# A diffusion ResBlock on one core: outer rows added by accumulating transfers in three more chunks, a wider weight nest, another order in the last unit

## The chip, the cores and the metric

The kernel runs on one core of one Trainium2 chip. The metric is the device time of one execution in microseconds, the median of several runs. A program's instructions go to TensorE (PE in the profile, its weight loads PEld), VectorE (DVE), ScalarE (ACT), GpSimd (POOL) and SyncE (SP). Each engine works through its own instructions in the order in which they stand in the program, and waits at an instruction whose inputs another engine has not finished. SP and POOL also issue transfers by the DMA engines; a transfer that adds to what lies at its destination is issued by POOL here.

## The reference

```python
# B, C, H, W = 2, 512, 64, 64; E = 1152; all inputs bfloat16
def gn(z, gamma, beta):                 # 4 groups of 128 channels, eps 1e-5
    zr = z.reshape(B, G, (C // G) * H * W)
    mu = zr.mean(-1).reshape(B, G, 1)
    var = ((zr - mu) ** 2).mean(-1).reshape(B, G, 1)
    zn = ((zr - mu) / jnp.sqrt(var + eps)).reshape(B, C, H, W)
    return zn * gamma.reshape(1, C, 1, 1) + beta.reshape(1, C, 1, 1)
def conv3(z, w):                        # 3x3, padding 1, the sum of nine taps
    zp = jnp.pad(z, ((0, 0), (0, 0), (1, 1), (1, 1)))
    taps = [jnp.einsum("bchw,oc->bohw", zp[:, :, i:i+H, j:j+W], w[:, :, i, j])
            for i in range(3) for j in range(3)]
    return sum(taps)
h = conv3(silu(gn(x, g1, be1)), w1)
h = h + (silu(t_emb) @ w_emb).reshape(B, C, 1, 1)
h = conv3(silu(gn(h, g2, be2)), w2)
return x + h
```

Two group norms, two 3x3 convolutions of 512 channels to 512 channels on two images of 64 x 64, an embedding and a residual.

## The kernel before

**The convolution.** It isn't computed tap by tap. Along the rows of the image it goes by a fast scheme: an output tile of four rows (at four interleaved positions) is made from six transformed planes of the input and six transformed weights. Planes 0 to 3 are the "middle points" and planes 4 and 5 the "outer points": plane 4 and plane 5 each give a part that belongs to only one of the four outputs (8 rows of the 32 that a chunk has, rows 24 to 31 and rows 0 to 7 of the tile as it is laid out). Along the columns a second, two-point nest saves a third of the matmuls of the middle points. VectorE makes the planes ("rows_a", "rows_b") from the activated input, and from the raw weights it makes the transformed ones.

**Chunks and units.** A chunk is one layer, one image and one half of the image's rows: eight chunks, 0 to 3 for the first convolution and 4 to 7 for the second. A unit is one chunk and one of four blocks of 128 output channels: 32 units, and their matmuls follow each other on TensorE in a fixed chain (`chain=True` in `mm`). A unit of chunks 4 to 6 has 88 matmuls: twelve of 512 columns for plane 4, 16 of 256 (B, points 0 and 2), twelve for plane 5, 16 (B, points 1 and 3), 16 (A, 0 and 2), 16 (A, 1 and 3). Chunk 7 nests the outer points too (Bo and Ao), so that all its 96 matmuls have 256 columns.

**After the matmuls.** ScalarE evacuates PSUM into float16 tiles: `evac_o` takes an outer point from bank 6 or 7 into the buffer OO, `evac_b` and `evac_pair` take two banks of the middle points (M, BT). PSUM has eight banks: 6 and 7 for the outer points, three pairs in turn for the middle ones. VectorE adds the B part (S, A in the names), takes sums and differences (s, d), ScalarE or VectorE scales (8, 2, 4), VectorE writes the 32 rows of the result to a buffer YS (y), and then the outer points are added to its rows 0 to 7 and 24 to 31 (O). There are two YS, used in turn, and in chunks 4 to 6 two OO, also in turn, at an offset in the weight regions (L970).

**How the outer points are added.** `CFG['oacc']` (L298) says it by chunk. Where it is 1 (chunks 0 to 2), one accumulating transfer on POOL's queue adds OO into YS; where it is 0, VectorE does it, in chunks 4 to 6 in two additions of 520 elements per partition (8 rows of 65):

```python
if CFG["oacc"][c] and not last:
    dma(yo.ap, oo.ap, [oo, yo], [yo], P * 4 * PL, nm + "oa", sw=True, acc=True)
elif md == "1":
    for i, r0 in ((1, 0), (0, 24)):
        r = A(ys + r0 * RW, [[1, PL]])
        tt(r, r, A(OO[i], [[1, PL]]), AD, nm + "O")
```

A unit of the second layer then stores YS to the output by another accumulating transfer on POOL's queue; the residual has been copied there before.

**The last chunk.** Before each unit of chunk 7, `nest_st` (L882) makes the nested weights of the outer points from the raw ones in six VectorE additions of 512 elements; the last of each half overwrites part of the raw weights. `unit7` (L890) runs B 0,2; B 1,3; the sums S of both; A 0,2; A 1,3; Bo; Ao. For the very last unit `last_y` (L1110) takes the place of the ending: it adds the residual x on VectorE, adds plane 5 straight from PSUM (L1142) and stores in three pieces on SP's queue.

**The order.** The whole program is recorded as a list of operations with planned durations, on five resources (PE, DVE, ACT, POOL, DMA). A list scheduler (`Plan._run`) then takes, at each step, the ready operation with the best priority, which fixes the order of every engine; `emit` writes the instructions in the order of planned start. The priorities come from a backward pass, corrected by a table of names (NUDGE) and by thirty seeded random moves (ORDER). POOL's transfers share a planned DMA resource with SP's, but on the chip they stand in POOL's own order, between its memsets.

Of the kernel before, what the change touches and what calls it, by code (L numbers as in the profile page):

```python
# [10 lines left out]
ACT = mybir.ActivationFunctionType  # L11
ALU = mybir.AluOpType
AX = mybir.AxisListType
F32 = mybir.dt.float32
BF16 = mybir.dt.bfloat16
# [6 lines left out]
class Op:  # L22
    __slots__ = ("i", "eng", "cost", "lat", "fn", "preds", "succs", "name", "start", "slack", "sw", "boost")


NUDGE = {
    ('a10', 'DMA'): -6.1,
    ('emb', 'DMA'): -4.9,
    ('k01', 'DVE'): 3.6,
    ('k10', 'DVE'): -17.9,  # L30
    ('ld_ur02', 'DMA'): -31,
    ('ld_ur11', 'DMA'): -12.6,
    ('ld_ur12', 'DMA'): 4.6,
    ('ld_ur13', 'DMA'): -26.7,
    ('ld_ur21', 'DMA'): -3.1,
    ('ld_ur23', 'DMA'): -69.1,
    ('ld_ur3', 'DMA'): -62.2,
    ('rob10', 'DVE'): -6,
    ('row11', 'DVE'): 19.2,
    ('silu00', 'ACT'): -8.7,  # L40
    ('silu11', 'ACT'): -0.4,
    ('st01', 'DVE'): 24.1,
    ('st02', 'ACT'): 36.2,
    ('st02', 'PE'): 26.8,
    ('st03', 'ACT'): 61.3,
    ('st10', 'ACT'): -3.4,
    ('st11', 'ACT'): -24.7,
    ('u004', 'DVE'): 81.3,
    ('u00d', 'DVE'): -4.5,
    ('u00y', 'DVE'): -1.5,  # L50
    ('u01m1', 'ACT'): -14.6,
    ('w1_00', 'DMA'): 12.8,
    ('w1_01', 'DMA'): -14.6,
    ('w1_03', 'ACT'): 45.4,
    ('w1_13', 'DVE'): 35.8,
    ('w1_20', 'DVE'): 27.3,
    ('w1_22', 'ACT'): 48.7,
    ('w1_22', 'DVE'): 67.4,
    ('w1_23', 'DVE'): 187.4,
    ('w1_31', 'ACT'): 16.7,  # L60
    ('w1_33', 'ACT'): 79.1,
}


ORDER = (2, (
    (204379228, 255, 30, 1),
    (234843898, 319, 120, 1),
    (211139775, 268, 30, 3),
    (669684967, 433, 15, 3),
    (1006773657, 341, 15, 3),  # L70
    (788794351, 91, 15, 3),
    (40166790, 349, 60, 1),
    (920935792, 232, 15, 1),
    (410399867, 107, 60, 0.3),
    (420875362, 192, 15, 1),
    (385567171, 251, 30, 3),
    (279912161, 95, 30, 0.3),
    (315890846, 329, 120, 1),
    (696499368, 218, 60, 1),
    (272137600, 194, 15, 0.3),  # L80
    (605732795, 129, 30, 1),
    (29479506, 139, 15, 1),
    (973994246, 204, 15, 1),
    (488781037, 250, 30, 1),
    (34394231, 99, 30, 0.3),
    (655024064, 49, 30, 0.3),
    (144588941, 58, 60, 0.3),
    (252865214, 352, 15, 1),
    (1046031975, 342, 30, 1),
    (242005847, 138, 15, 1),  # L90
    (974414065, 143, 15, 1),
    (73604465, 212, 30, 3),
    (659385421, 129, 15, 1),
    (738286652, 264, 120, 3),
    (573361134, 368, 15, 1),
))


class Plan:
# [118 lines left out]
    def solve(self, rounds=3):  # L218
        ops = self.ops
        n = len(ops)  # L220
        tail = [0.0] * n
        for o in reversed(ops):
            tail[o.i] = o.cost + max((tail[s] + self.edge_lat(o, ops[s]) for s in o.succs), default=0.0)
        pri = [-t for t in tail]
        pris, best = [], None
        for k in range(rounds):
            pris.append(pri)
            st, span = self._run(pri, False)
            if k + 1 == rounds:
                break  # L230
            bt, bspan = self._run([-(s + o.cost) for s, o in zip(st, ops)], True)
            pri = [-(b + o.cost) for b, o in zip(bt, ops)]
        k, moves = ORDER
        pri = np.array(pris[k]) - np.array([NUDGE.get((o.name, o.eng), 0.0) for o in ops])
        st = np.array(self._run(pri.tolist(), False)[0])
        for seed, t0, w, sg in moves:
            pri = pri + np.where((st >= t0) & (st < t0 + w), np.random.default_rng(seed).normal(size=n) * sg, 0.0)
        best = self._run(pri.tolist(), False)
        self.span = best[1]
        for o, s in zip(ops, best[0]):  # L240
            o.start = s
        return best
# [26 lines left out]
def _idx(off, dims):  # L269
# [8 lines left out]
PL = 8 * RW  # L278
# [6 lines left out]
BB, CT, P, NCH, ET = 2, 4, 128, 2, 9  # L285
# [6 lines left out]
CFG = {  # L292
    'k0': (D_, D_, D_, D_),
    't0': D_,
    'k': (D_, D_, A_, D_, A_, A_, A_, A_),
    't': (D_, D_, A_, D_, A_, A_, A_, A_),
    's': ((D_, D_, D_), (D_, D_, D_), (D_, A_, A_), (D_, D_, D_), (A_, A_, A_), (A_, A_, A_), (A_, A_, A_), (D_, A_, D_)),
    'oacc': (1, 1, 1, 0, 0, 0, 0, 0),  # L298
    'np': 1,
    'st0': ('DA', 'DA', 'DP', 'PP'),  # L300
    'warm': 9,
    'bact': 1,
    'push': (40.0, 0.0, 0.0, 0.0),
    'vacc': (0, 1, 1, 1, 1, 1, 1, 0),
# [4 lines left out]
def kernel(  # L309
# [14 lines left out]
    o = 0  # L324
    UREG, UM = [], 10304
# [57 lines left out]
    def A(off, dims, dt=None):  # L383
        b = ar[:] if dt is None else ar[:].bitcast(dt)
        n = 1
        for d in dims:
            n *= d[1]
        return R(bass.AP(b.tensor, b.offset + off, [list(b.ap[0])] + [list(d) for d in dims]),
                 ("A", _idx(off, dims)), n)
# [32 lines left out]
    def tt(out, a, b, op, name=""):  # L422
        return pl.op("DVE", 0.075 + 0.000521 * out.n, lambda: nc.vector.tensor_tensor(out=out.ap, in0=a.ap, in1=b.ap, op=op),  # L423
              regs(a, b), regs(out), name)
# [40 lines left out]
    def mm(lst, name="", chain=True, slack=2.5, boost=0.0, warm=1.0):  # L465
        rr, ww, cost = [], [], 0.0
        for out, lhsT, rhs, st, sp in lst:
            rr += [lhsT, rhs]
            ww.append(out)
            cost += {512: 0.2195, 256: 0.109, 384: 0.166}.get(rhs.n, max(0.0715, rhs.n / 2330.0)) * warm  # L470

        def fn():
            for out, lhsT, rhs, st, sp in lst:
                ins = nc.tensor.matmul(out.ap, lhsT=lhsT.ap, rhs=rhs.ap, start=st, stop=sp, skip_group_check=True)  # L474
            return ins
        pl.op("PE", cost, fn, regs(*rr), regs(*ww), name, chain=chain, slack=0.0 if chain else slack, boost=boost)
# [113 lines left out]
    def st_off(s, ct):  # L590
        return UREG[2 * s + ct // 2] + 8192 + (ct % 2) * 768
# [107 lines left out]
    LV = VB[0]  # L699
# [38 lines left out]
    SB_, AD = ALU.subtract, ALU.add  # L738
# [79 lines left out]
    ucnt = [0]  # L818
# [46 lines left out]
    def Bo_mms(bank, c, k, ct, s):  # L865
        lst = []
        for q in range(2):
            w = (A(LV + 4160 + ucnt[0] % 2 * 1024 + ct * 256 + (s - 4) * 128, [[1, 128]]) if q == 0 else
                 A(st_off(ucnt[0] % 2, ct) + (s - 4) * 384 + 128, [[1, 128]]))
            lst.append((Ps(bank, q * 256, [[1, 256]]), w, A(onest(ct, 3 - q, s), [[1, 256]]),  # L870
                        ct == 0 and q == 0, ct == CT - 1 and q == 1))
        return lst
# [7 lines left out]
        return lst  # L880

    def nest_st(s, nm):  # L882
        for h in range(2):
            g = lambda kx, dt=BF16: A(st_off(s, 2 * h) + kx * 128, [[384, 4], [1, 128]], dt)
            t = A(LV + 3136 + h * 512, [[128, 4], [1, 128]])
            tt(t, g(0), g(2), ALU.add, nm)
            tt(A(LV + 4160 + s * 1024 + h * 512, [[128, 4], [1, 128]]), t, g(1), ALU.add, nm)
            tt(g(1, None), t, g(1), ALU.subtract, nm)

    def unit7(c, k):  # L890
        nm = f"u{c}{k}"
# [3 lines left out]
        last = u == 31  # L895
        BT, SD = BT1, SD1
# [5 lines left out]
        def run(steps):  # L902
            for (bank, s, fn) in steps:
                for ct in range(CT):
                    mm(fn(bank, c, k, ct, s), nm + f"{fn.__name__[0]}{s}")

        def evac_b(s, bank):
            act(A(BT + s * 512, [[1024, 2], [1, 512]]), Ps(bank, 0, [[512, 2], [1, 512]]), ACT.Copy, scale=0.5 * KAP[s], name=nm + "b")

        def evac_pair(s, bank):  # L910
            act(M(s, 2, 1024), Ps(bank, 0, [[512, 2], [1, 512]]), ACT.Copy, scale=KAP[s], name=nm + f"m{s}")

        row = lambda base, r0, dt=None: A(base + r0 * RW, [[RW, 8], [33, 2], [1, 32]], dt)
        nest_st(u % 2, nm + "n")
        run([(p1, 0, B_mms), (p1 + 1, 2, B_mms)])
        evac_b(0, p1)
        run([(p2, 1, B_mms), (p2 + 1, 3, B_mms)])
        evac_b(1, p2)
        g = lambda q: A(BT + q * 256, [[512, 4], [32, 8], [1, 32]])
        for o, op in ((0, AD), (32, SB_)):  # L920
            tt(A(SD + o, [[512, 4], [64, 8], [1, 32]]), g(0), g(1), op, nm + "S")
        run([(p3, 0, A_mms), (p3 + 1, 2, A_mms)])
        evac_pair(0, p3)
        run([(p4, 1, A_mms), (p4 + 1, 3, A_mms)])
        evac_pair(1, p4)
        run([(p5, 4, Bo_mms), (p5 + 1, 5, Bo_mms)])
        for i, sc in enumerate((0.5, 0.125)):
            act(A(BO + i * 512, [[1, 512]]), Ps(p5 + 1 - i, 0, [[1, 512]]), ACT.Copy, scale=sc, name=nm + "b")
# [17 lines left out]
        tt(A(ys, [[RW, 32], [33, 2], [1, 32]]), A(MB, [[SD - MB, 2], [0, 2], [1, 512]]),  # L946
           A(MB + 1536, [[SD - MB - 512, 2], [-512, 2], [1, 512]]), AD, nm + "y")
        yo = A(ys, [[24 * RW, 2], [1, PL]])
        tt(yo, yo, A(OS, [[PL, 2], [1, PL]]), AD, nm + "O")
        tt(yo, yo, A(OA, [[PL, 2], [1, PL]]), AD, nm + "O")  # L950
        yv = A(ys, [[1, YF]])
        b, ch = chunks[c][1:]
        dma(out[b, k, ch], yv.ap, [yv], [K("o", b, k, ch, i) for i in range(2)], P * YF * 2, nm + "out", sw=True, acc=True)
# [493 lines left out]
```

## Time and profile before

| | us |
|---|---|
| median of 5 runs | 457.53 |
| lowest and highest of them | 456.85 and 462.34 |
| the profiled execution | 456.85 |
| its span, first to last instruction | 454.8 |
| TensorE busy | 441.3 |
| VectorE busy | 432.4 |
| ScalarE busy | 391.7 |
| POOL busy | 63.4 |

The mean granted clock of TensorE is 0.992. The six transfer groups of the profile that matter here: outer rows and plane sums added in SBUF by POOL's queue, 30 transfers of 260 KB; results added to the output, 15 of 520 KB; the residual copied to the output, 30 of 260 KB; raw weights of the second layer, 28 of 192 KB; the stored activations read back, 16 of 520 KB; the last stores, one of 260 and two of 130 KB.

In the profile's rows, L423 is the line of `tt`, so all two-input VectorE operations carry it; L427 is `ts`, L446 `act`, L459 `dma`, L463 `memz`, L474 the matmuls. So one goes by shapes: 128x520 on VectorE is an outer addition of chunks 4 to 6, 128x512 from bf16 is the weight nest, 128x2048 the y rows. The columns of a group are: line, engine, operation, tiles, shapes, count | busy us, mean ns of one | idle us of the engine just before them and what ended it. Successive VectorE instructions overlap a little, so a group's busy time is less than the count times the mean.

### The profile page before, as it was taken

How to read it: one execution, taken by the hardware profiler on the slowest of the kernel's cores; microseconds unless marked ns; L12 is line 12 of the kernel's file. 1: busy time of each engine (PE TensorE's matmuls, PEld its weight loads, DVE VectorE, ACT ScalarE, POOL GpSimd, SP SyncE). 2: the span in 40 equal slices, each digit the busy share in tenths (PEclk: the TensorE clock that was granted, in tenths of full speed). 3: DMA queues.
4: the chain of work that ended last, by engine and by line, in shares of the span. 5: the costliest groups of instructions: out<-in, count | busy, mean ns of one | idle time of the engine just before them, and what ended most of it. 6: DMA issues, size and time to landing. Idle time of an engine off the chain costs nothing. (4 is left out here: it accounts for less than half of the span.)

```text
span 454.8 us, 8314 instructions
## 1 busy us (share of the span) xinstructions
PE 441.3 (97%) x2866; PEld 277.7 (61%) x2866; DVE 432.4 (95%) x865; ACT 391.7 (86%) x620; POOL 63.4 (14%) x94
## 2 busy tenths in 40 slices
PE   6899999999999999999999999999999999999993
PEld 4654444456555555555555566777666667788883
DVE  4899999999999999979999999998999999999997
ACT  5989999999999997799995899859997999567663
POOL 2110020112110221112110001121121111011211
PEclk9899999999999999999999999999999999999998
DMA  8974479979887788987996757858884864363844
GB/s 323 397 242 119 137 199 269 257 189 281 277 205 224 220 208 241 257 263 251 268 363 225 247 193 207 212 144 179 200 206 93 199 194 101 100 165 49 194 86 94
DMA packets 45977, 94.10 MB, mean 207 GB/s; under 512 B 7024, under 2 KB 18160, under 8 KB 45936
## 3 DMA queue, kind: packets, MB, share of 16 engines
q1 hardware_dynamic: 35712, 77.60, 50.9%
q0 software_dynamic: 9936, 15.98, 22.6%
q8 instruction: 22, 0.36, 0.3%
q14 instruction: 19, 0.16, 0.1%
q10 hardware_dynamic: 288, 0.01, 0.0%
HBM read 62.25 MB, written 31.32 MB: 206 GB/s over the span
## 5 line engine op out<-in xcount | busy, mean ns | idle before, releaser
L474 PE MATMUL psum<-ar 128*128 128x256 f16 (+2 forms) x2739 | 427.6, 319 | 1.5 <-DVE ar L423 1.0
L423 DVE TENSOR_TENSOR ar<-ar 128x1024 f16<-128x1024 f16 (+6 forms) x692 | 403.2, 650 | 10.3 <-ACT ar L446 6.8
L474 PEld LDWEIGHTS <-ar 128*128 128x128 f16 (+1 forms) x2775 | 267.7, 98 | 160.2 <-issue 2.5
L446 ACT ACTIVATE ar<-ar 128x512 f16<-128x512 f16 (+6 forms) x204 | 181.6, 926 | 19.2 <-DVE ar L423 15.3
L446 ACT ACTIVATE ar<-psum 128x512 f16<-128x512 f32 (+3 forms) x227 | 157.6, 726 | 31.2 <-PE psum L474 16.8
L446 ACT ACTIVATE ar<-ar,fs 128x2112 f16<-128x2112 f16 (+3 forms) x36 | 70.8, 1973 | 0.7 <-DMA ar<-in_x_dram 0.6
L459 POOL DMA_DIRECT2D ar<-ar x30 | 30.5, 1040 | 161.9 <-DVE ar L423 71.7
L459 POOL DMA_DIRECT2D out_dram<-ar x15 | 18.2, 1210 | 94.5 <-DVE ar L423 94.5
L427 DVE TENSOR_SCALAR ar<-ar 128x512 f16<-128x512 f16 (+4 forms) x74 | 24.9, 350 | 0.0
L446 ACT ACTIVATION_READ_ACCUMULATOR ar<-psum 128x1 f32 x96 | 22.0, 229 | 0.0
L463 POOL MEMSET ar<- 128x65 f16 (+6 forms) x30 | 5.9, 240 | 80.7 <-DVE ar L423 35.3
L446 ACT ACTIVATION_READ_ACCUMULATOR ar<-ar 128x1 f32 x50 | 10.5, 211 | 0.0
L474 PE MATMUL psum<-ar,ones_bf 128*128 128x260 bf16 x40 | 6.1, 303 | 2.7 <-DMA ar<-in_x_dram 2.1
L1188 DVE BATCH_NORM_STATS2 fs<-ar 128x6 f32<-128x416 bf16 x15 | 8.0, 581 | 0.0
L567 POOL TENSOR_TENSOR fs<-fs 128x4 f32<-128x4 f32 x3 | 4.0, 1347 | 21.5 <-DVE fs L555 21.5
L474 PEld LDWEIGHTS psum<-fs,ones_neg 128*128 128x128 f32 x42 | 5.7, 191 | 2.1 <-DVE fs L1192 0.7
L474 PEld LDWEIGHTS <-ones_bf 128*128 128x128 bf16 x40 | 4.1, 107 | 4.2 <-issue 2.7
L474 PE MATMUL psum<-fs,ones_neg 128*128 128x1 f32 (+3 forms) x42 | 5.4, 242 | 0.9 <-DVE fs L1192 0.6
L559 POOL TENSOR_TENSOR fs<-fs 128x1 f32<-128x1 f32 x4 | 3.0, 744 | 21.2 <-DVE fs L555 21.2
L489 PE MATMUL psum<-ones_bf 128*128 128x512 bf16 x9 | 3.6, 582 | 1.1 <-DVE ones_bf L480 1.1
L545 DVE TENSOR_SCALAR fs<-psum 128x2 f32<-128x2 f32 x4 | 0.6, 159 | 3.9 <-PE psum L474 3.4
L446 ACT ACTIVATE fs<-fs 128x1 f32<-128x1 f32 x4 | 1.5, 384 | 1.9 <-POOL fs L560 1.9
(46 smaller groups left out, 19.9 us busy)
## 6 DMA issues: line engine op xcount, KB each, us to landing
ar<-in_w_dram SPq DMA_DIRECT2D x32, 384.0 KB, 4.6
ar<-in_x_dram SPq DMA_DIRECT2D x16, 552.5 KB, 5.0
h_scr<-ar SPq DMA_DIRECT2D x16, 520.0 KB, 3.3
ar<-h_scr SPq DMA_DIRECT2D x16, 520.0 KB, 3.7
out_dram<-in_x_dram SPq DMA_DIRECT2D x30, 260.0 KB, 3.9
ar<-ar POOLq DMA_DIRECT2D x30, 260.0 KB, 4.9
out_dram<-ar POOLq DMA_DIRECT2D x15, 520.0 KB, 6.1
u_scr<-ar SPq DMA_DIRECT2D x16, 384.0 KB, 3.6
```

What stands on the lines that cost most here:

```text
L423: return pl.op("DVE", 0.075 + 0.000521 * out.n, lambda: nc.vector.tensor_tensor(out=out.ap, in0=a.ap, in1=b.ap, op=op), regs(a, b), regs(o ...
L427: pl.op("DVE", cost or 0.075 + 0.00026 * out.n, lambda: nc.vector.tensor_scalar(out=out.ap, in0=a.ap, scalar1=s, scalar2=None, op0=ALU.mul ...
L446: lambda: nc.scalar.activation(out=out.ap, in_=a.ap, func=func, scale=sc, **kw), regs(*rr), regs(*ww), name)
L459: lambda: eng.dma_start(out=out, in_=in_, **kw), regs(*r), regs(*w), name, lat=lat or (3.2 if sw else None), after=after, sw=sw)
L463: pl.op("POOL" if eng == "gpsimd" else "DVE", 0.08 + 0.0005 * out.n, lambda: e.memset(out.ap, v), (), regs(out), name)
L474: ins = nc.tensor.matmul(out.ap, lhsT=lhsT.ap, rhs=rhs.ap, start=st, stop=sp, skip_group_check=True)
L489: nc.tensor.matmul(psum[:, 0:512], lhsT=ones_bf[:], rhs=wr, start=True, stop=True, skip_group_check=True)
L545: pl.op("DVE", 0.16, lambda: V.tensor_scalar(out=F(tot, 2 * n).ap, in0=ps.ap, scalar1=YF / HW, scalar2=None, op0=ALU.mult), regs(ps), regs ...
L559: nc.gpsimd.tensor_tensor(out=N.ap, in0=N.ap, in1=F(NEGH, n).ap, op=ALU.pow)
L567: pl.op("POOL", 0.85 if n == 1 else 1.9, lambda: nc.gpsimd.tensor_tensor(out=F(rs, n).ap, in0=N.ap, in1=F(NEGH, n).ap, op=ALU.pow), regs(N ...
L1188: pl.op("DVE", 0.07 + 0.00104 * d.n, lambda d=d, i=i: V.bn_stats(out=F(BNS + 6 * i, 6).ap, in_=d.ap), regs(d), regs(F(BNS + 6 * i, 6)), name)
```

## The change

Five edits:

1. `oacc` becomes 1 for chunks 4, 5 and 6: the two additions of 520 in each of their twelve units become one accumulating transfer of 128 x 2 x 520 elements on POOL's queue.
2. `nest_st` works on all four input blocks at once: three additions of 1024 elements in place of six of 512. The third result goes to a place of its own (offset 10496), and `Bo_mms` reads it there; the raw weights are no longer overwritten.
3. In the last unit the middle points go in pairs: B 0,2; its sums; A 0,2; then B 1,3; its sums; A 1,3; Bo and Ao follow as before. The sums S are four operations of 512 elements there, in place of two of 1024.
4. The planner's priorities: the backward pass, NUDGE and ORDER go, and one number for each recorded operation stands in a table PRI. The planned duration of a 512-column matmul goes from 0.2195 to 0.2202.
5. A switch `o7` is added that could add the outer points of chunk 7 by transfer; it is (0, 0), so nothing of it is used.

```diff
-NUDGE = {
...
-ORDER = (2, (
...
+PRI = (
+    3890, 4301, 4467, 4151, 4299, 4149, 4525, 4510, 4474, 4467, 4462, 4457, 4453, 4446, 4443, 4461, 4465, 4447, 4440, 4436, 4433, 4426, 4420, 4409,
...
+)
@@ Plan.solve
-        pris, best = [], None
-        for k in range(rounds):
...
-        best = self._run(pri.tolist(), False)
+        assert len(PRI) == n
+        best = self._run([-p / 10.0 for p in PRI], False)
@@ CFG
-    'oacc': (1, 1, 1, 0, 0, 0, 0, 0),
+    'oacc': (1, 1, 1, 0, 1, 1, 1, 0),
...
+    'o7': (0, 0),
@@ mm
-            cost += {512: 0.2195, 256: 0.109, 384: 0.166}.get(rhs.n, max(0.0715, rhs.n / 2330.0)) * warm
+            cost += {512: 0.2202, 256: 0.109, 384: 0.166}.get(rhs.n, max(0.0715, rhs.n / 2330.0)) * warm
@@ Bo_mms
-            w = (A(LV + 4160 + ucnt[0] % 2 * 1024 + ct * 256 + (s - 4) * 128, [[1, 128]]) if q == 0 else
-                 A(st_off(ucnt[0] % 2, ct) + (s - 4) * 384 + 128, [[1, 128]]))
+            w = A(LV + (10496 if q else 4160) + ucnt[0] % 2 * 1024 + ct * 256 + (s - 4) * 128, [[1, 128]])
@@ nest_st
-        for h in range(2):
-            g = lambda kx, dt=BF16: A(st_off(s, 2 * h) + kx * 128, [[384, 4], [1, 128]], dt)
-            t = A(LV + 3136 + h * 512, [[128, 4], [1, 128]])
-            tt(t, g(0), g(2), ALU.add, nm)
-            tt(A(LV + 4160 + s * 1024 + h * 512, [[128, 4], [1, 128]]), t, g(1), ALU.add, nm)
-            tt(g(1, None), t, g(1), ALU.subtract, nm)
+        g = lambda kx: A(st_off(s, 0) + kx * 128, [[UM, 2], [384, 4], [1, 128]], BF16)
+        n = lambda o: A(LV + o, [[512, 2], [128, 4], [1, 128]])
+        tt(n(3136), g(0), g(2), ALU.add, nm)
+        tt(n(4160 + s * 1024), n(3136), g(1), ALU.add, nm)
+        tt(n(10496 + s * 1024), n(3136), g(1), ALU.subtract, nm)
@@ unit7
+        def s_ops(i, st, n):
+            for o, op in ((0, AD), (32, SB_)):
+                g = lambda q: A(BT + i * 512 + q * 256, [[st, n], [32, 8], [1, 32]])
+                tt(A(SD + i * 512 + o, [[st, n], [64, 8], [1, 32]]), g(0), g(1), op, nm + "S")
+
+        if last:
+            for i, b_, a_ in ((0, p1, p2), (1, p3, p4)):
+                run([(b_, i, B_mms), (b_ + 1, i + 2, B_mms)])
+                evac_b(i, b_)
+                s_ops(i, 1024, 2)
+                run([(a_, i, A_mms), (a_ + 1, i + 2, A_mms)])
+                evac_pair(i, a_)
+        else:
...
+            s_ops(0, 512, 4)
...
```

In the built program VectorE has 34 operations fewer (24 additions, 12 of the nest, and two sums more), POOL has twelve transfers more, each standing ahead of its unit's store, and TensorE has the same matmuls, in another order within the last unit. The order of the other operations differs from before in few places in the first chunks and in more of them from chunk 4 on.

## The prediction

> **What bounds the kernel now.** I read the busy shares first, then the idle time of TensorE, then of VectorE, then the end of the trace.
>
> The head of the page:
>
> ```profile
> span 454.8 us, 8314 instructions
> PE 441.3 (97%) x2866; PEld 277.7 (61%) x2866; DVE 432.4 (95%) x865; ACT 391.7 (86%) x620; POOL 63.4 (14%) x94
> ```
>
> Two engines are nearly full, so one must see where each is the limit. The timeline of TensorE alone, its last two rows (start, length, what, idle before), and its waits from 36 us on:
>
> ```profile
> 295.43 35.66 PE L474 MATMUL psum<-ar 128*128 128x512 f16 x258
> 331.56 115.96 PE L474 MATMUL psum<-ar 128*128 128x512 f16 x912 [0.47 <-ACT ar L446]
> ...
> PE psum L474 <- ACT ar L446: 0.5, 1, 0.5
> ```
>
> From 36 us to its last matmul at 447.5 us TensorE idles visibly once, 0.47 us. No matmul is added or removed. So only three places can give time: the first 36 us, that stall (with 0.08 us more between 406 and 447 us in the table by stretches), and the 7.3 us from 447.5 to 454.8.
>
> VectorE's waits, first for 323 to 452 us, then for 256 to 323 us:
>
> ```profile
> DVE ar L423 <- issue: 0.6, 1, 0.6
> ...
> DVE ar L423 <- ACT ar L446: 2.8, 4, 1.4
> ```
>
> VectorE is full through chunks 5 to 7, but it is TensorE that is never late for long: VectorE's queue is long, not limiting. That changes at the end. The timelines there, ScalarE, then VectorE, then the output transfers:
>
> ```profile
> 444.06 1.51 ACT L446 ACTIVATE ar<-psum 128x1024 f16<-128x1024 f32 x2 [0.72 <-PE psum L474]
> 445.81 0.60 ACT L446 ACTIVATE ar<-psum 128x512 f16<-128x512 f32 x1 [0.23 <-PE psum L474]
> 446.69 0.60 ACT L446 ACTIVATE ar<-psum 128x512 f16<-128x512 f32 x1 [0.28 <-PE psum L474]
> 447.32 1.92 ACT L446 ACTIVATE ar<-ar 128x512 f16<-128x512 f16 x3
> ...
> 442.69 8.43 DVE L423 TENSOR_TENSOR ar<-ar 128x1024 f16<-128x1024 f16 x18
> 451.04 0.68 DVE L1142 TENSOR_TENSOR ar<-ar,psum 128x512 bf16<-128x512 f16 x1
> ...
> 449.32 2.76 SPq L459 DMA_DIRECT2D out_dram<-ar  x3
> ```
>
> VectorE ends at 451.72, 4.2 us after TensorE, and the last store and the program's end take 3.1 us more.
>
> **The change, part by part.** Durations come from one execution of 456.85 us (span 454.8 and 2.05 around it); the median of five is 457.53, 0.68 more.
>
> *Outer rows by transfer.* In each of the 12 units of chunks 4 to 6, two VectorE additions go and one accumulating transfer on POOL's queue comes. The groups:
>
> ```profile
> L423 DVE TENSOR_TENSOR ar<-ar 128x520 f16<-128x520 f16 x60 | 24.4, 423 | 0.1
> L459 POOL DMA_DIRECT2D ar<-ar x30 | 30.5, 1040 | 161.9 <-DVE ar L423 71.7 <-issue 20.9 <-PE psum L474 20.9
> ar<-ar POOLq DMA_DIRECT2D x30, 260.0 KB, 4.9
> ```
>
> VectorE's instructions overlap: 692 of 0.650 us are 449.8 us, but L423 is busy 403.2 us, so each costs 0.067 less than its length, 0.36 us for this form. 24 x 0.36 = 8.6 us leave VectorE. Nearly all of it lies beside TensorE and is worth nothing there by itself. What it can do is remove the stall. At 331.56 TensorE waited for ScalarE, and ScalarE waits for VectorE 22.1 us in 21 places between 256 and 447 us, against 12.9 us for TensorE. With VectorE earlier by 0.7 us per unit I count both stalls as gone: **-0.55 us** (bounds 0 and -0.55).
>
> The price is a new wait. The buffer of the outer rows (OO, two sets) is written again two units later by the opening evacuation (o4) on ScalarE. Before, it was free when VectorE had added it. Now it is free when the transfer lands: 4.9 us in the median (3.3 to 8.4 over the 30, 3.3 to 5.6 over the six after 260 us), beside 0.3 us until POOL issues. ScalarE works in order, so behind a late o4 stand the next evacuations, the SiLU and the scalings of the next chunk, and behind those VectorE. Three places by today's times: the unit opened at 331.6 us evacuates at 335.8, and the rows its transfer adds into are written at 333.2, so it would land at 333.2 + 0.3 + 4.9 = 338.4, 2.6 us late. The next: 345.3 + 5.2 = 350.5 against 347.2, 3.3 late. The buffer written at 380.4: 385.6 against 384.1, 1.5 late. The two reuses between these are on time by 0.4 and 0.7, those before 320 us at most 0.8 late. The cover: TensorE's opening bank is next written a unit less its own 12 matmuls later, 12.2 - 2.6 = 9.6 us, and an evacuation pair's bank after 6.1 us (one plain run of 2.6 and two pair runs of 16 x 0.110). A late o4 of 4 us fits into both if ScalarE catches up. Its room by stretch (TensorE, weights, VectorE, ScalarE, POOL busy):
>
> ```profile
> 331.00:344.00 13.00, 12.53 (x90) 8.71 (x89) 13.00 (x19) 13.00 (x15) 3.07 (x5) 1.00 0.83 198
> 344.00:356.00 12.00, 12.00 (x88) 8.42 (x87) 12.00 (x18) 8.31 (x13) 1.21 (x1) 1.00 0.53 109
> 356.00:368.00 12.00, 12.00 (x88) 8.36 (x86) 11.21 (x19) 12.00 (x13) 1.53 (x3) 1.00 0.76 210
> 368.00:381.00 13.00, 13.00 (x95) 9.15 (x94) 13.00 (x22) 12.90 (x15) 1.21 (x1) 1.00 0.59 145
> ```
>
> From 331 to 381 us ScalarE has 3.8 us free of 50. Yet in the same profile ScalarE is full in three of these four stretches, with one stall of 0.47 us for it. Bounds for the new wait: 0, and +8.5 us if each landing takes the 6.1 us of the stores in the same queue (3.8 + 4.5 + 2.7 + 0.5 + 0.8 = 12.3 us late, 3.8 of it free). At 4.9 us it is 7.4 late less 3.8, and VectorE writes each of the three late buffers 0.7 us earlier: 1.5. I take **+0.25**, half of the one stall seen, because the banks' cover stands before all of this, and that stall is the nearest row to what gets through.
>
> POOL: an issue costs it 1.04 us, 12 x 1.04 = 12.5 us beside 391 us idle. But the result's store stands behind the transfer in POOL's queue and blocks it for some 4.9 us per unit. Behind it are the next chunk's accumulations (3 a chunk) and two zeroed rows. Their waits today are 3 to 8 us long, for work far ahead of its use, so I take 0 (bounds 0 and +0.5, the size of one stall seen). In the DMA engines the 30 transfers and 15 stores of that queue take 22.6%: 103 engine-us per MB, so 12 x 0.27 MB is 330 of 2336 engine-us between 256 and 402 us, 14% on top of 0.35 to 0.90. Loads are issued ahead of use; 0 again.
>
> The Trainium skill, "DMA: Bandwidth & Descriptors", section "Anatomy of one DMA", fits a POOL transfer as 2.0 us plus bytes over 436 GB/s; an estimate from that is 2.6 us for these 266 KB, and the three late places would be 0.3, 1.0 and on time. The measured 4.9 us decides; that row is of accumulating transfers, which the fit doesn't name. The same skill, "SBUF — State Buffer", section "Who interferes with whom", speaks against POOL transfers beside VectorE copies and scalings, which can lock out the writing of descriptors; here the longest of the 30 issues took 1.47 us beside a full VectorE.
>
> *Weight nest.* Six additions of 512 become three of 1024 in four units: 6 x 0.36 - 3 x (0.69 - 0.07) = 0.3 us each, 1.2 us. It ends up in VectorE's slack. The third result has a new place, so it waits for chunk 6's last matmuls (405 us) and is needed some 7 us later: 0.
>
> *Last unit.* Its matmuls change places among themselves; the pair 1,3 still ends 32 matmuls (3.5 us) before the end, at 444.0. Two sums of 1024 become four of 512: 4 x 0.36 - 2 x 0.62 = +0.2 us on VectorE, before the end. After the last evacuation of that pair (444.06 + 1.02 = 445.08) stands a chain. Now: its additions at 445.3, but the x addition stands before the sums, and ScalarE scales at 447.32, 447.86 and 448.6. After, by the built program's order, the x additions stand ahead: addition 445.3 to 446.0, two differences to 446.7, ScalarE's first two scalings 446.85 to 448.0, the evacuation o4 to 448.55, the last scaling to 449.15, VectorE's row 449.3 to 449.7, then 1040, 512 and the PSUM row (0.70, 0.43 and 0.68 less overlaps) to 451.4. That is **-0.3 us** against 451.72. VectorE can be there in time: in its gapless stretch from 365 us on, five pairs of outer additions (5 x 0.72) and the nest (1.2) go, 4.8 us. Bounds: 0, if VectorE is as late as now, and -3.4, when only the PSUM addition is left behind the last matmul (447.5 + 0.15 + 0.68 = 448.3).
>
> *The written-out priorities.* They replace a computed order. In the first 36 us the order on all engines is the same but for a few neighbours changed, so 0 (bounds -0.3 and +0.3, one or two steps of 0.36 us moved less a part beside others).
>
> **Sum:** -0.55 + 0.25 - 0.3 = -0.6, so 456.25 against 456.85, and with the 0.68 to the median 456.9 us.
>
> **The rivals.**
> *The transfer's landing becomes ScalarE's wait and TensorE's stall.* Place: o4 of the units opened between 331 and 381 us. For it: ScalarE full there, 7.4 us of lateness at today's times. Against it: the earlier VectorE, and the banks' cover of 6 to 9.6 us. It decides from 3.8 us of added lateness on. Price 1.5 to 8.5 us, less 0.3 at the end: 457.53 + 1.2 to + 8.2, so 458.7 to 465.7.
> *VectorE's relief arrives at the end in full.* For it: VectorE is gapless to the end. Against: the chain behind 445.08 above. -0.55 - 3.4: 453.6.
> *It does nothing that can be seen:* another engine covers the stall and the end keeps its length: 457.5.
>
> **How the numbers follow.** Forecast, 455.9 to 457.9: 0.60. Nothing, 457 to 458: 0.12. ScalarE's wait, 458.7 to 465.7: 0.20. Full relief, 453.3 to 455: 0.08. The forecast and the nothing case overlap. The range 454.5 to 461.0 leaves out half of each outer case. 1% (4.6 us), about what a measurement of this kernel can tell from no change, is under 453.0 or over 462.1: faster 0.03, slower 0.09, within 0.88.
>
> **What would show it.** Right: VectorE's busy time near 423 us, with gaps for ScalarE in chunks 5 to 7; TensorE's stall at 331 gone, no new one over 0.5 us; TensorE ending between 446.5 and 447.5 and VectorE some 4 us behind; ScalarE waiting for transfers ar<-ar by 1 to 4 us in several places. Wrong: TensorE waiting for ScalarE several times after 300 us (first rival), or VectorE ending within 2 us of TensorE (second), or the first 36 us shifted by more than 0.3.

## The result and the profile after

The changed kernel takes 462.41 us, median of its runs (457.15 to 467.77), beside 457.91 us (455.03 to 463.88) for the kernel before on the same chips: a ratio of **1.0073, interval 1.0056 to 1.0090**. By that ratio it is 3.3 us slower, by the two medians 4.5; the forecast was 456.9 us in a range of 454.5 to 461.0. One thing is needed to read all that follows: executions of either kernel fall into two groups some 4 us apart, for a reason ahead of the changed code (last section), and the ratios leave out executions over 1.5% above the fastest of their kernel.

The profiled execution took 461.91 us. From its page, the head, TensorE's largest group and the accumulating transfers inside SBUF:

```profile
span 460.1 us, 8286 instructions
...
PE 441.6 (96%) x2866; PEld 277.6 (60%) x2866; DVE 424.6 (92%) x831; ACT 392.2 (85%) x620; POOL 77.7 (17%) x106
...
L506 PE MATMUL psum<-ar 128*128 128x256 f16 (+2 forms) x2739 | 427.8, 319 | 6.6 <-ACT ar L478 5.3
...
ar<-ar POOLq DMA_DIRECT2D x42, 260.0 KB, 4.8
```

VectorE was relieved as forecast (432.4 to 424.6 us), and the transfers' median is still 4.8 us. But TensorE, with the same busy time, now waits 5.3 us for ScalarE, where it had waited 0.5. Its timeline near the places (start, length, what, idle before and its releaser), the last row from a wider window:

```profile
329.83 8.79 PE L506 MATMUL psum<-ar 128*128 128x256 f16 x53
340.23 3.65 PE L506 MATMUL psum<-ar 128*128 128x256 f16 x32 [1.61 <-ACT ar L478]
345.81 3.45 PE L506 MATMUL psum<-ar 128*128 128x256 f16 x23 [1.92 <-ACT ar L478]
...
384.65 15.72 PE L506 MATMUL psum<-ar 128*128 128x256 f16 x111 [1.78 <-ACT ar L478]
```

The timeline of ScalarE where the first of these begins:

```profile
338.24 1.94 ACT L478 ACTIVATE ar<-psum 128x1024 f16<-128x1024 f32 x2 [2.40 <-DVE ar L455]
```

and of VectorE ahead of that:

```profile
325.02 4.55 DVE L455 TENSOR_TENSOR ar<-ar 128x2048 f16<-128x2048 f16 x6
335.73 2.42 DVE L455 TENSOR_TENSOR ar<-ar 128x2048 f16<-128x2048 f16 x2 [6.17 <-DMA ar<-ar]
```

Read from the bottom: VectorE, the relieved engine, stands still for 6.17 us, waiting for a transfer; ScalarE then waits for VectorE; TensorE waits for ScalarE, twice. It waits a third time from 382.9 us on; whether that stall belongs to the same chain is taken up below. By the starts of successive matmuls the three cost 1.8, 2.1 and 1.9 us. In the kernel before, VectorE runs without a gap there:

```profile
321.30 23.99 DVE L423 TENSOR_TENSOR ar<-ar 128x1024 f16<-128x1024 f16 x33
```

Which transfer? The instruction behind the gap is a plane operation ("rows_b", 128x2048) of chunk 6 that overwrites the rows which the accumulation of chunk 6's first plane block reads. So it may not start before that accumulation has landed. POOL's queue around it, after:

```profile
316.48 1.20 POOL L491 DMA_DIRECT2D ar<-ar  x1 [3.75 <-DVE ar L455]
320.82 0.15 POOL L495 MEMSET ar<- 128x65 f16 x1 [3.15 <-ACT ar L478]
324.93 1.21 POOL L491 DMA_DIRECT2D out_dram<-ar  x1 [3.96 <-DMA ar<-ar]
325.66 1.40 POOL L491 DMA_DIRECT2D ar<-ar  x1
329.49 0.86 POOL L491 DMA_DIRECT2D ar<-ar  x1 [2.43 <-issue]
```

and before:

```profile
317.41 1.21 POOL L459 DMA_DIRECT2D out_dram<-ar  x1 [5.11 <-DVE ar L423]
321.85 0.90 POOL L459 DMA_DIRECT2D ar<-ar  x1 [3.23 <-PE psum L474]
```

The first line after is the new transfer of unit 4,3's outer rows (chunk 4, fourth block of channels). The store of that unit stands behind it and waits 3.96 us for its landing (the third line's releaser, "DMA ar<-ar"); the accumulation stands behind the store. The same three by issue and landing:

| | before | after |
|---|---|---|
| outer rows of 4,3 | (VectorE) | 316.48 to 324.64, 8.2 us |
| store of 4,3 | 317.41 to 323.86 | 324.93 to 333.60 |
| accumulation, chunk 6, first block | 321.85 to 325.23, 3.4 us | 325.66 to 335.64, **10.0 us** |
| VectorE starts the operation that waits for it | 330.76 | 335.73 |

The accumulation is issued 3.8 us later and takes 6.6 us more to land, 10.4 in all. It had been 5.5 us early (325.23 against 330.76); VectorE, relieved, is there 1.2 us sooner (329.56). 10.4 - 5.5 + 1.2 = 6.1 us, the gap. This is theory Q (the queue).

### The profile page after: what moved, and what is told of

It is laid out like the page before. It is cut to its first block, busy times and chain, and to the rows that moved or that the text cites. A ratio compares the mean times of both kernels' runs of the same rounds, so it can differ in the third digit from the quotient of the medians.

```text
span 460.1 us, 8286 instructions
## 1 busy us (share of the span) xinstructions
PE 441.6 (96%) x2866; PEld 277.6 (60%) x2866; DVE 424.6 (92%) x831; ACT 392.2 (85%) x620; POOL 77.7 (17%) x106
## 5 line engine op out<-in xcount | busy, mean ns | idle before, releaser
L455 DVE TENSOR_TENSOR ar<-ar 128x1024 f16<-128x1024 f16 (+7 forms) x658 | 395.3, 665 | 23.0 <-ACT ar L478 12.5
L491 POOL DMA_DIRECT2D ar<-ar x42 | 45.5, 1099 | 195.7 <-DVE ar L455 119.0
L478 ACT ACTIVATION_READ_ACCUMULATOR ar<-psum 128x1 f32 x96 | 23.2, 241 | 0.0
```

The source lines that it names most:

```text
L478: lambda: nc.scalar.activation(out=out.ap, in_=a.ap, func=func, scale=sc, **kw), regs(*rr), regs(*ww), name)
L491: lambda: eng.dma_start(out=out, in_=in_, **kw), regs(*r), regs(*w), name, lat=lat or (3.2 if sw else None), after=after, sw=sw)
```

## The experiments

In each the order of every engine is written out as the scheduler had made it, and only the steps shown are edited; a diff shows the steps of a queue in their order. "4,3" is chunk 4, fourth unit. The theories: **Q**, the order of POOL's queue as above; **A**, the prediction's first rival, that ScalarE's opening evacuation waits until the outer rows have left their buffer; **O**, that the new order or the other parts of the change cost by themselves. Ratios are to the kernel before, with 95% intervals:

| run | edit | ratio |
|---|---|---|
| e1 | after, store of 4,3 behind two accumulations | 1.0054 (1.0032 to 1.0075) |
| e8 | ... behind the outer rows of 5,0 too | 0.9991 (0.9957 to 1.0026) |
| e9 | after, no store of 4,3 | 0.9978 (0.9937 to 1.0019) |
| e2 | after, outer rows of 4,3 on VectorE | 0.9994 (0.9961 to 1.0026) |
| e3 | before, outer rows of 4,3 by transfer | 1.0020 (0.9995 to 1.0046) |
| e5 | before, all twelve by transfer | 1.0049 (0.9973 to 1.0126) |
| e6 | after, outer rows left out | 1.0001 (0.9960 to 1.0043) |
| e4 | after, all twelve on VectorE | 1.0148 (1.0102 to 1.0195) |
| e10 | e4 with the additions 4 to 5 us later | 1.0130 (1.0055 to 1.0206) |
| e11 | e1 and a buffer of its own for 5,0 | 1.0041 (1.0000 to 1.0082) |
| e12, e16 | before, with nest and last unit only | 1.0043 (1.0008 to 1.0077), 1.0059 (1.0021 to 1.0097) |
| e13, e17 | after, unedited | 0.9998 (0.9958 to 1.0037), 1.0024 (0.9981 to 1.0067) |
| e14 | as e8 | 1.0037 (0.9995 to 1.0079) |
| e15, e18 | as e2 | 0.9985 (0.9948 to 1.0022), 0.9983 (0.9946 to 1.0020) |

### Taking the store out of the way

```diff
 outer rows of 4,3        (transfer)
-store of 4,3
 accumulation, chunk 6, block 0
 accumulation, chunk 6, block 1
+store of 4,3              # e1
 outer rows of 5,0        (transfer)
+store of 4,3              # e8, in place of the line above
```

> The changed kernel with every engine's order kept, but for one transfer: on POOL's queue the store of unit 4,3 stands behind the first two plane accumulations of chunk 6 instead of ahead of them. Theory Q (the store waits in POOL's in-order queue for the landing of the outer rows, and the plane accumulation behind it comes too late): the 6.2 us gap of VectorE near 330 us goes, TensorE loses under 1 us there, ratio to the kernel before 0.996 to 1.001. Theory A (ScalarE's evacuations wait for the OO buffer until the transfer lands): all these waits are still there, ratio 1.005 to 1.009. Theory O (the new priorities' order is worse by itself): 1.005 to 1.009.

> The changed kernel with the store of unit 4,3 moved further back on POOL's queue: behind both plane accumulations and behind the outer rows of unit 5,0. Then none of the three has the 520 KB store ahead of it. Theory Q (what stands behind a store in POOL's queue lands late): plane accumulation and outer rows land 3 to 5 us after their issue, no stall over 1 us near 330 to 345 us, 0.996 to 1.000. If the store's own delay hurts (the two stores then follow each other): 1.002 to 1.006.

In e1 the gap at 330 us is gone: the accumulation lands 4.0 us after its issue (321.76 to 325.78) while 4,3's outer rows are as slow as before (7.9 us). That part of Q holds. But the store, now at 330.35, blocks what is behind it in its new place: the outer rows of 5,0, issued at 332.49, land at 342.32, 9.8 us later, and ScalarE waits for them. ScalarE's waits of e1 from 323 to 400 us show theory A at work:

```profile
ACT ar L1578 <- DMA ar<-ar: 6.9, 3, 4.5
```

So A was no fiction: it needs a slow queue. TensorE lost 2.2 us at 342, and 1.7 more at 381. With the store behind that transfer too (e8) its outer rows land in 3.8 us, and the ratio is 0.9991. TensorE's waits from 36 us on, e8:

```profile
PE psum L1606 <- ACT ar L1578: 1.9, 2, 1.4
```

e11 gave 5,0's outer rows a buffer of its own in e1's order:

```diff
 # order of e1
-outer rows of 5,0 in OO, second set
+outer rows of 5,0 in a place that nothing uses then
```

> The run with the store of unit 4,3 behind two plane accumulations (1.0054), with the outer rows of unit 5,0 in a buffer of their own, so that the opening evacuation of unit 5,2 no longer waits for their transfer. In that run ScalarE waited 4.5 us there, for a landing 9.8 us after the issue. If this wait is the rest of the loss: ratio 0.996 to 1.001, and no stall of TensorE over 1 us near 342 us. If not: 1.004 to 1.007.

1.0041 lies at the edge of both answers. The wait near 342 and TensorE's stall behind it are gone, so the buffer did what it should; but ScalarE then waits 4.3 us for a landing at 354, one unit later, and TensorE loses 2.5 us at 381.6, its only stall after the head. A buffer for one unit passes the wait on to the next. (e7, with e1's order, gave all units a third buffer in turn, in a place that the second layer's sums use as well; its 1.0305, 1.0234 to 1.0377, mixes the two uses.)

Leaving the store out (one quarter of one chunk's result isn't written):

```diff
-store of 4,3
```

> The changed kernel in its order, with the store of unit 4,3 left out (that block of the output keeps only the residual). All twelve transfers of outer rows stay. Theory Q: the plane accumulation goes out about 4 us earlier and lands in 4 to 5 us in place of 10, the 6.2 us gap of VectorE near 330 us goes, 0.995 to 1.000. Theories A and O: 1.005 to 1.009.

0.9978: no gap, one stall of 1.1 us behind the head. And leaving the cause out, with the store where it was:

```diff
-transfer: YS += outer rows of 4,3
+VectorE: two additions of 520
```

> The changed kernel in its order, with the outer rows of one unit alone (4,3) added by VectorE again, in two additions; the other eleven units keep their transfers. Theory Q: the store of 4,3 waits for nothing long, the plane accumulation goes out in time: 0.996 to 1.002. Theory A: eleven of twelve waits stay, and the one that goes (unit 5,1's evacuation, 8 us after the landing) was none: 1.005 to 1.009. Theory O: 1.005 to 1.009.

0.9994, with **one transfer of twelve** back on VectorE. All other parts of the change and the new order are in this kernel, so theory O is not the loss. VectorE's timeline of e2 has no gap there:

```profile
319.02 27.50 DVE L1555 TENSOR_TENSOR ar<-ar 128x1024 f16<-128x1024 f16 x38 [1.40 <-ACT ar L1578]
```

From e2's waits between 300 and 400 us:

```profile
ACT ar L1578 <- DMA ar<-ar: 6.6, 4, 2.5
...
PE psum L1606 <- ACT ar L1578: 0.3, 1, 0.3
```

ScalarE still waits 6.6 us for landing outer rows in four places, and TensorE hardly notices, which fits the cover of the banks that the prediction counted on.

### From the other side

```diff
 # order of the kernel before
-VectorE: two additions of 520      # unit 4,3 (e3); all twelve units (e5)
+transfer: YS += outer rows
```

> The kernel before in its order, with the outer rows of unit 4,3 alone added by a transfer that is issued right after its y rows. Theory Q: this one transfer carries most of the loss, a gap of VectorE of 3 to 6 us near 330 us, ratio 1.004 to 1.010. Theory A: the buffer is used again 14 us later, no wait: 0.999 to 1.001. Theory O: 0.999 to 1.001.

> The kernel before in its own order, with all twelve transfers of outer rows in place of the additions, each issued right after its y rows: the first part of the change alone. Theory Q (POOL's queue): what stands behind a store lands late here too; ratio to the kernel before 1.002 to 1.010, between the one transfer of unit 4,3 alone (1.002) and more. Theory O (the loss needs the new order): 0.997 to 1.001.

e3 missed its size: 1.0020. Its profile says why. The outer rows landed 5.9 us after their issue, the accumulation behind the store in 7.9 (at 331.5), and VectorE, not relieved elsewhere, came to its operation at 331.0: a gap of 0.7 us. All twelve (e5) brought the whole picture into the old order: outer rows of 4,3 in 7.4 us, the accumulation 12.0 us after its issue, a gap of 6.35 us on VectorE and 3.1 us on TensorE behind it. Its ratio gives no verdict: it rests on two executions (460.3 and 464.9 us), while the other eight took 469.6 to 472.3, some 2% over the kernel before. So a loss by the queue doesn't need the new order; but here the twelve cost far more than 4,3 alone, with four more stalls of 0.6 to 1.2 us in the profile, and what the other eleven do in the old order wasn't taken apart.

### What the relief is worth

```diff
-transfer: YS += outer rows         # twelve units
+                                   # e6: nothing (rows 0 to 7 and 24 to 31 lack the outer points)
+VectorE: two additions of 520      # e4: right behind y;  e10: 4 to 5 us later
```

> The changed kernel in its order, with the outer rows of chunks 4 to 6 left out altogether, neither transferred nor added (the rows 0 to 7 and 24 to 31 of those twelve results lack their plane 4 and plane 5 part). It shows what VectorE's relief is worth without any price. Theories Q and A: no gap of VectorE over 3 us between 320 and 350 us, no stall of TensorE over 1 us after 300 us, ratio to the kernel before 0.995 to 0.999. Theory O (the order is worse by itself): 1.003 or more.

> The changed kernel in its order, with the outer rows of all twelve units of chunks 4 to 6 added by VectorE again; the wide nest, the last unit's order and the new priorities stay. Theories Q and A: the loss goes, 0.998 to 1.002. Theory O: the loss stays, 1.005 to 1.009.

> The changed kernel in its order, with the outer rows of chunks 4 to 6 added by VectorE as in the run that cost 1.5%, but the two additions of each unit 4 to 5 us later in VectorE's order, just ahead of the store's place. If that run was slow because of where the additions stood (straight behind y, ahead of what ScalarE waits for): 0.999 to 1.005. If the new order has no room for them on VectorE at all: 1.010 to 1.018.

With neither additions nor transfers, VectorE simply waits for ScalarE. Its waits in e6 from 256 to 447 us, where the kernel before had 2.8 us:

```profile
DVE ar L1543 <- ACT ar L1566: 8.5, 8, 2.5
```

The ratio is 1.0001: beside the kernel before, the 8.6 us taken from VectorE bring nothing that can be measured, though theories Q and A gave them 0.1 to 0.5%. e4 missed all theories: with the additions back TensorE stalls in six places of 0.8 to 1.8 us, and placing them later (e10; there some of them read a buffer after its next use) changed nothing. The new order has no room for them on VectorE: it needs the relief, and brings nothing measurable in return.

### Nest and last unit alone

```diff
 # order of the kernel before
-nest in six additions; B 0,2; B 1,3; S; A 0,2; A 1,3
+nest in three; B 0,2; S; A 0,2; B 1,3; S; A 1,3        # last unit
```

> The kernel before with the second and third part of the change alone: the wide weight nest in chunk 7 and the last unit's new order; outer rows of chunks 4 to 6 on VectorE as before. VectorE's end comes 3.7 to 3.9 us behind TensorE's last matmul in place of 4.2, so 0.3 to 0.5 us are gained: ratio 0.997 to 1.001. If VectorE's relief is needed for that, the end stays at 4.2 or more: 0.999 to 1.003.

> The kernel before with the wide nest and the last unit's order alone. If these parts cost nothing and the 1.0043 measured came from POOL's operation of 4.5 us (0.7 us in other executions) at 29 us, which stands in both kernels' code: 0.996 to 1.001. If they cost by themselves: 1.003 to 1.006, and in a profile without the long POOL operation TensorE ends 1.5 to 3 us later than before.

Slower twice. Part is a long operation on POOL in the head, which both profiles have (last section); the rest is at the end. From TensorE's last matmul to VectorE's last row pass 5.6 us in both, against 4.2 before and 3.8 after. ScalarE's timeline at the end, e12, then after:

```profile
452.94 1.15 ACT L1580 ACTIVATE ar<-ar 128x512 f16<-128x512 f16 x2 [2.34 <-DVE ar L1557]
```

```profile
452.39 1.15 ACT L478 ACTIVATE ar<-ar 128x512 f16<-128x512 f16 x2 [0.48 <-DVE ar L455]
```

VectorE, still with its 24 additions, lets ScalarE wait 2.3 us before the last scalings. So the new ending seems to need the relief (its order was copied from the changed kernel; another may do better).

### On one chip

The changed kernel and the two cures were measured again side by side, e13 to e16 on one chip, e17 and e18 on another.

> The changed kernel with its order written out as a table, nothing edited, beside the three next on one chip. If the place of unit 4,3's store in POOL's queue is the loss: 1.005 to 1.010 as measured before, VectorE's gap of some 6 us at 330 us, TensorE's stalls at 338, 344 and 383 us. If the loss depended on the chip: 0.997 to 1.003.

> The changed kernel with the store of unit 4,3 behind two plane accumulations and the transfer of unit 5,0, beside the unedited one on one chip. If the store's place is the loss: 0.997 to 1.003, and lower than the unedited kernel by 0.5% or more. If the parts left in it (nest, last unit, the new order) cost 0.4% by themselves: 1.003 to 1.006.

> The changed kernel with only unit 4,3's outer rows added by VectorE again, beside the unedited one on one chip. If the transfer that its store waits for is the loss: 0.997 to 1.003, and lower than the unedited kernel by 0.5% or more. If the other eleven transfers cost as well: 1.003 or more.

> The changed kernel with its order written out as a table, nothing edited, once more beside the next on one chip. In the last comparison 8 of its 12 executions took what the kernel before takes, and the profiled one lost 4 us. If the loss is decided in each execution by how late the outer rows of unit 4,3 land: 1.000 to 1.010; a profiled execution with the gap of 5 to 6 us on VectorE near 330 us has those rows landing 7.5 us or more after their issue, one without it sooner.

> The changed kernel with only unit 4,3's outer rows added by VectorE again, beside the unedited one on one chip. If the transfer that its store waits for is the loss: 0.996 to 1.001 whatever the unedited kernel gives, no gap over 3 us on VectorE near 330 us. If the loss is another: it follows the unedited kernel within 0.2%.

The unedited kernel gave 0.9998, below its expectation, and 1.0024, with 1 inside both intervals, so the loss isn't there in every execution. By the medians of all executions it was 2.4 and 1.2 us over the kernel before (461.01 against 458.66, 462.34 against 461.16), the kernel with 4,3 on VectorE 0.8 us under it and level with it (457.88, 461.21). All executions of all comparisons by their time:

| | under 459.5 us | 459.5 to 463 | over 463 |
|---|---|---|---|
| before (209) | 126 | 76 | 7 |
| after (68) | 11 | 30 | 27 |
| 4,3 on VectorE: e2, e15, e18 (34) | 19 | 15 | 0 |
| store behind 5,0: e8, e14 (22) | 9 | 10 | 3 |

On the two chips of e13 to e18 alone the rows are 26, 28, 4 before; 7, 9, 8 after; 12, 12, 0 with 4,3 on VectorE. By the profiles of kernels without the loss (last section), the two groups of the kernel before are those without and with the long POOL operation. The counts fit a changed kernel that adds some 4 us to both in most executions, not in all. With 4,3 on VectorE the groups are those of before again. Moving the store (e8) repeats only halfway: 0.9991 on one chip, 1.0037 on another.

All three profiled executions of the changed kernel are of the losing kind, so none shows a run without the loss; they show its steps in different sizes:

| | outer rows of 4,3 land after | gap on VectorE | the two stalls of TensorE behind it | the third stall |
|---|---|---|---|---|
| first profile | 8.2 us | 6.2 us | 3.9 us | 1.9 us |
| e13 | 7.6 us | 4.9 us | 2.6 us | 2.8 us |
| e17 | 6.8 us | 4.2 us | 1.9 us (one stall) | 3.1 us |

The gap and the stalls right behind it follow the landing. The third stall goes the other way, and kernels without the gap have one in that place too: 1.6 us in e8 and e14, 1.7 in e1, 2.5 in e11, 1.2 in e18, 0.4 in e15, none in e2 and e9. TensorE's timeline of e8:

```profile
381.38 18.79 PE L1606 MATMUL psum<-ar 128*128 128x256 f16 x133 [1.45 <-ACT ar L1578]
```

So the order of the queue is shown to cost 1.9 to 3.9 us of TensorE in these profiles, and how much of the third stall it makes is open (in e17 ScalarE had waited 2.0 us for landing outer rows just ahead of it, as in theory A). That the executions without loss are those where the rows of 4,3 land sooner still is likely, not shown.

## Why the prediction was wrong

**The step that failed** is "Behind it are the next chunk's accumulations (3 a chunk) and two zeroed rows ... for work far ahead of its use, so I take 0 (bounds 0 and +0.5, the size of one stall seen)". The block was seen, and what was queued behind it was named, but not looked up: the accumulation's landing and its first use were in the trace of before, 325.23 and 330.76, 5.5 us ahead. The block was put at 4.9 us, the median, which just fits into that. Two terms were missing. The rows of this one transfer took 6.8 to 8.2 us, near the upper end of the 3.3 to 8.4 that the prediction had read. Why so long isn't shown: while they were under way, from 316 to 325 us, the DMA engines' share was 0.72, against 0.91 before. And a transfer behind a store of 520 KB lands behind it: 10.0 us instead of 3.4. With both, in place of 0 the step comes to 4.2 to 6.2 us of VectorE and, in these profiles, 1.9 to 3.9 us of TensorE in the stalls right behind it (4.9 to 5.8 with the third stall, whose share is open).

**The stalls (-0.55).** Not confirmed. The one near 415 us went, also in e2; the one at 331 came back in most profiles of cured kernels (0.5 us in e2, 0.6 in e8, 0.8 in e14, 0.9 in e15, not in e18). e6 bounds the relief itself at 0.9960 to 1.0043. VectorE's queue was long, not limiting, as the prediction's own reading of the waits said; by that reading the term should have been 0.

**ScalarE's wait for the buffer (+0.25).** The size stands where no store blocks POOL's queue: with 6.6 us of such waits, TensorE waited for ScalarE 0.3 us in e2. Rival A's price came up only in e1, where a store stood ahead. The measured time lies in that rival's range, and its sign (TensorE waiting for ScalarE several times after 300 us) came, but by another way: through POOL's queue to VectorE, not through the buffer to ScalarE. That the rival's number fits is luck.

**The last unit (-0.3).** After, 3.8 us from the last matmul to VectorE's end, against 4.2: -0.43, as forecast. It is 3.8 to 3.9 in e8, e13 to e15, e17 and e18 too. In all these TensorE's stalls after 300 us make 1.2 us or more, by which VectorE may have gained time. In e2, almost without them, it is 4.8 us, and ScalarE waits 1.5 us for VectorE: +0.6, over the upper bound of 0.

**The nest, the first 36 us, VectorE's busy time** came out as forecast: nothing from the nest in after or e2, the first long run of matmuls at 35.84 against 35.61 us, 424.6 us against "near 423".

**The rule of the Trainium skill** on POOL's transfers ("DMA: Bandwidth & Descriptors", section "Anatomy of one DMA") would give an estimated 2.6 us for these 266 KB; the shortest landing here took 3.3 us, and the one that mattered 8.2. On the lock-out of descriptors ("SBUF — State Buffer", "Who interferes with whom") the longest issue of an accumulating transfer in the stretch took 1.40 us, which doesn't account for landings of 8 to 10.

## What to carry to other kernels

Before a transfer is put into an in-order queue ahead of something that waits for it, list everything behind that wait with its landing and first use, and price the block with the longest landing seen there and with what stands ahead of it in the queue, not with the median. VectorE, busy but not limiting, gave nothing back when it was relieved; ask first what an engine will wait for then. When one place of twelve costs most, as in the new order here, leave that one as it was: e2 is as fast as the kernel before, though none of these kernels beats it.

## What the runs showed of the hardware

**POOL's transfers land in the order of issue.** In the twenty profiles, with 45 to 57 such transfers each, none landed ahead of an earlier one, whatever their sizes; in the three profiles of the changed kernel the accumulation issued 0.7 us behind the store of 4,3 landed 1.5 to 2.0 us after it, and 9.3 to 10.0 us after its own issue. In other kernels too, where it was issued 0.7 us behind that store, it landed 6.3 to 12.0 us after its issue (e2, e3, e5, e15, e18); with no store issued in the 4 us ahead of it, 3.3 to 4.3 us (before, e1, e8, e9, e11, e14). The Trainium skill ("DMA: Bandwidth & Descriptors", "Queues, rings and completion order") says of transfers that SyncE and ScalarE issue that descriptors are consumed in ring order on each DMA engine, and that completion is not in the order of issue; for POOL's transfers here the rows look like the first half, and a case of the second didn't occur.

**One POOL operation has two lengths.** An operation of the first group norm in the head, a power of a 128x1 column, takes 0.68 us in some executions and 4.47 in others, in both kernels' code. POOL's timeline of the kernel before, and of e12:

```profile
29.16 0.68 POOL L559 TENSOR_TENSOR fs<-fs 128x1 f32<-128x1 f32 x1 [4.00 <-DVE fs L555]
```

```profile
29.27 4.47 POOL L1693 TENSOR_TENSOR fs<-fs 128x1 f32<-128x1 f32 x1 [3.99 <-DVE fs L1689]
```

Behind the long one ScalarE and VectorE wait, and TensorE idles 2.8 to 3.0 us near 36 us. At its restart, or up to 1.1 us later, the granted clock goes to 0.5 for 3.4 us, and eight matmuls of 512 columns take 427 ns each instead of 219. The length of the idle time alone doesn't decide that: after 2.9 us at 343 us in e5 the same came 1.1 us later (sixteen matmuls of 256 columns at 213 instead of 109 ns), after 2.9 us at 384 us in e17 it didn't. The idle time and the slow matmuls make 2.8 + 8 x 0.21 = 4.5 us. Profiled executions of kernels without the loss took 456.9 to 459.5 us with the short operation (before, e2, e3, e6, e8, e15) and 461.3 to 463.7 with the long one (e9, e12, e14, e16, e18): the two groups of times. What makes the operation long isn't shown.
